# Fourth block of a retention-plus-MLP kernel: its chunks loaded in quarters, its first scores and k^T v' issued together

## The chip, the cores and the metric

One core of a Trainium2 chip. The metric is the device time of one execution in microseconds (us), the median of several runs. All time differences below are small beside the whole, so the profile is read in hundredths of a microsecond.

## The reference

Two stages in float32. The first is a recurrent retention over 768 tokens, for 4 batches and 8 heads of width 64; its output, 3072 tokens by 512, goes into an MLP with an ELU between its two layers.

```python
gamma = 1.0 - 2.0 ** (-5.0 - np.arange(H, dtype=np.float32))
for t in range(S):
    state = gamma[None, :, None, None] * state + np.einsum('bhd,bhe->bhde', k[:, :, t], v[:, :, t])
    y[:, :, t] = scale * np.einsum('bhd,bhde->bhe', q[:, :, t], state)
...
h = x @ w_in
g = np.where(h > 0.0, h, alpha * (np.exp(np.minimum(h, 0.0)) - 1.0))
return (g @ w_out).astype(np.float32)
```

## The kernel before

**Tiling.** The 3072 tokens are 24 chunks of 128 and six blocks of 512 (four chunks each, CPB = 4). The recurrence is computed in parallel form: per chunk, scores (q times k within 64 tokens, masked), states (sums of k^T v', where v' is v scaled by powers of gamma), and outputs. These matmuls use 64x64 tiles of the TensorE array; all MLP products use 128x128 tiles. The MLP's products are Strassen-like (seven products for eight), so each layer is a row of "products" that gather in PSUM banks named a, b and d, with sums by VectorE and copies by ScalarE between them.

**Order.** The order of every engine's instructions is the order of the program text (a manual schedule; no planner). Generators yield at certain points, and the loop around them puts side work into these points. The stage of the change is the second layer of the second block: `second_twice` (L954) runs seven outer products j in `ORDER2` (L804), each of seven inner products of 0.89 us. In its loop (L1802) every j from the second on gives three points, called "first", "middle" and "end" of a step; steps count from 1. From "first" to "middle" two products run, from "middle" to "end" one, from "end" to the next "first" four.

**Side work at these points.** The outputs of the third block's retention (`VISITS`, L1800), the loads of the fourth block's chunks (`LOADS`, L1801), and the fourth block's first pair of chunks: `scores(3, 0)` (L1818) at the end of step 4 and `states(3, 0)` (L1820) at the end of step 5. A run of 64x64 matmuls between 128x128 products is a visit. `scores` (L336) makes 64 profiled matmuls into two PSUM tiles, which VectorE masks into the chunk's k area; `states` (L385) makes 64 into two more and sums them (one copy by ScalarE, three additions by VectorE) in the chunk's area of plain k. All four PSUM tiles come from the pool of four, `ps_r` (L92).

**Chunks.** A chunk is a tile of 128 partitions x 2048 floats (1 MB): columns 0 to 1023 are q and k, turned; 1024 to 1535 are v; 1536 to 2047 are plain k. `load` (L114) takes one of four buffers (`ldpool`, L86) and issues the DMA on SP's queue (L125); `scale_v` (L299) scales v on GpSimd (POOL).

**Weights.** The weights of each inner product, 256 KB, come through a ring of 11 slots (L1776, L1777). When a product is issued, `done` (L857) frees its slot and `fetch` (L850) issues the next load, so a block is asked for about eleven products ahead. These loads, the chunk loads and the stores share SP's one queue, in program order. DMA completions are counted on eight semaphores in turn, and SP waits for the DMA issued eight before on the same one.

Of the kernel before, what the change touches and what calls it, by code (L numbers as in the profile page):

```python
# [28 lines left out]
def kernel(  # L29
# [47 lines left out]
    CPB = TB // C  # L77
# [34 lines left out]
    raw = {}  # L112

    def load(m, cuts=(0, 2048), behind=None):  # L114

        if m >= NCHUNK:
            return
        t = ldpool.tile([P, 2048], FP32, name="chunk", tag="chunk")
        raw[m] = (
            t[:, 0:1024].rearrange("p (a h c) -> p a h c", a=2, c=C),  # L120
            t[:, 1024:2048].rearrange("p (a h d) -> p a h d", a=2, d=D),
        )
        hold(t, behind)
        for lo, hi in itertools.pairwise(cuts):
            nc.sync.dma_start(t[:, lo:hi], qkv[m, :, lo:hi])  # L125

    def hold(t, other):

        if other is not None:
            nc.gpsimd.tensor_copy(t[0:1, 0:1], other[0:1, 0:1])  # L130
# [144 lines left out]
    powers_of(slice(0, 2 * C))  # L275

    load(0, (0, 1024, 1536))
    parts = load_piece_parts(2)
    next(parts)
    load(1, (0, 1536))  # L280
    next(parts, None)
    load_piece(staged[0][:, :, 0].bitcast(FP32))
    load(2, behind=raw[1][0][:, 0, 0])
    load(3, behind=staged[0][:, 512:, 0].bitcast(FP32))
    load_piece(staged[1][:, :, 0].bitcast(FP32))
# [13 lines left out]
    def scale_v(m, by_vector=False):  # L299
        if m >= NCHUNK:  # L300
            return
        i = chunks[m][1]
        v = raw[m][1][:, 0]
        eng = nc.vector if by_vector or m < 2 else nc.gpsimd
        eng.tensor_tensor(  # L305
            out=v, in0=v, in1=vf[:, i].unsqueeze(2).to_broadcast([C, H, D]), op=ALU.mult
        )
# [28 lines left out]
    def scores(tb, pp):  # L336

        sc = [ps_r.tile([P, 2, HP, D], FP32, name="sc", tag="r") for _ in range(2)]
        for x in range(2):
            score_products(sc, tb, pp, x)  # L340
        for a in range(2):
            nc.vector.tensor_tensor(
                out=raw[tb * CPB + 2 * pp + a][0][:, 1].rearrange("p h c -> p (h c)").rearrange("p (n t) -> p n t", t=D),
                in0=sc[a].rearrange("p x h t -> p (x h) t"),
                in1=cmask.unsqueeze(1).to_broadcast([P, 2 * HP, D]), op=ALU.mult,
            )
# [38 lines left out]
    def states(tb, pp):  # L385

        kvs = [ps_r.tile([P, 2, HP, D], FP32, name="kv", tag="r") for _ in range(2)]
        for x in range(2):
            state_products(kvs, tb, pp, x, range(2))
        for x in range(2):  # L390
            for sub in range(2):
                state_sum(kvs, tb, pp, x, sub)
# [284 lines left out]
    def send_small(count=None):  # L677
        for _ in range(min(count or len(to_send), len(to_send))):
            nc.sync.dma_start(*to_send.pop(0))
# [165 lines left out]
    def sent(j):  # L845
        send_small()
        blocked.discard((2, "t", j))
        fetch()
# [770 lines left out]
    def some(steps, count):  # L1619
        for _ in itertools.islice(steps, count):  # L1620
            pass
# [77 lines left out]
    def retention_step(tb, step):  # L1699
        if step == 0:  # L1700
            scores(tb, 0)
            scores(tb, 1)
        elif step == 1:
            states(tb, 0)
            states(tb, 1)
        else:
            outputs_step(tb, step - 2)
# [90 lines left out]
    flush()  # L1798
    retention_step(2, 2)
    step, VISITS = 0, {(1, "first"): 3, (1, "end"): 4}  # L1800
    LOADS = {(1, "first"): 0, (2, "end"): 1, (4, "end"): 2, (5, "end"): 3}  # L1801
    for s in sec:  # L1802
        if s == "first":
            step += 1
        at = (step, s if s in ("first", "middle") else "end")
        if s in ORDER2 and 1 <= step <= 4:
            some(smalls[1], 1 if step < 4 else 3)
        if step == 5:
            send_small(2)
        elif at == (6, "first"):  # L1810
            sent(1)
        if at in VISITS:
            retention_step(2, VISITS[at])
        if at in LOADS:
            load(3 * CPB + LOADS[at])
            scale_v(3 * CPB + LOADS[at])
        if at == (4, "end"):
            scores(3, 0)  # L1818
        elif at == (5, "end"):
            states(3, 0)  # L1820
        if s == ORDER2[-1]:
            break
# [8 lines left out]
    for nb in range(NB):  # L1831
# [40 lines left out]
        def bring(tb, n):  # L1872
            load(tb * CPB + n)
            scale_v(tb * CPB + n)
# [160 lines left out]
        step = 0  # L2035
# [3 lines left out]
        ]  # L2039
        LOADS = [(3, "middle"), (3, "end"), (4, "first"), (4, "middle")]  # L2040
        for s in sec:
# [5 lines left out]
            at = (step, s if s in ("first", "middle") else "end")  # L2047
            if more and at in VISITS:
                n = VISITS.index(at)
                retention_step(groups[n // 5], n % 5)  # L2050
            if more and at in LOADS:
                bring(groups[1], LOADS.index(at))
            if s == BIG2[-1]:
# [57 lines left out]
```

## Time and profile before

| what | value |
|---|---|
| median of 3 runs | 608.93 us (608.89 to 610.05) |
| the profiled execution | 609.02 us |
| its span | 607.2 us |
| TensorE busy | 600.0 us (99%) |
| VectorE / ScalarE / POOL busy | 507.7 / 261.5 / 97.4 us |
| DMA moved | 139.85 MB, 230 GB/s on average |
| HBM read / written | 105.12 / 33.82 MB |
| granted TensorE clock | 1.00 |

The span runs from the first to the last instruction; the profiled execution's time is 1.8 us longer. Times within the profile are counted from the span's start. PE is TensorE's matmul side, PEld its weight loads, DVE is VectorE, ACT ScalarE, SP the engine that issues all DMAs here. A line of the chain of waits reads: start in us, duration in us, engine, tile written, source line, number of instructions; "issue" in place of an engine is time in which the engine waited for nothing that the profile shows. A row for a stretch of time reads: from, to, length, then each engine's busy us and count, the granted clock, the share of time that the 16 DMA engines were busy, and GB/s. "DMA to landing" is the time from the issue of a DMA on SP to its completion. [...]

### The profile page before, as it was taken

The numbers are of one execution on the slowest core, as the hardware profiler recorded it, in microseconds if no ns is written. First come the engines' busy times: TensorE is split into PE (matmuls) and PEld (weight loads), VectorE is DVE, ScalarE is ACT, GpSimd is POOL, SyncE is SP. The second block draws the span as 40 slices with busy tenths as digits, with TensorE's granted clock in tenths as the row PEclk, the third lists the DMA queues.
The fourth block names the chain that finished last, engine by engine and source line by source line (L and its number), as shares of the span: only waits on it lengthen the run. The fifth ranks groups of instructions, "written<-read, shape, count | busy, mean of one in ns | idle before, by whom it ended". The sixth has DMA issues, their size and how long they took to land.

```text
span 607.2 us, 13751 instructions
## 1 busy us (share of the span) xinstructions
PE 600.0 (99%) x5510; PEld 492.7 (81%) x5510; DVE 507.7 (84%) x779; ACT 261.5 (43%) x448; POOL 97.4 (16%) x77
## 2 busy tenths in 40 slices
PE   8999999999999999999999999999999999999997
PEld 6865568888889999888766888888888866788886
DVE  5779889989899877989898787898658999779785
ACT  6898734205553112147589310100136679611110
POOL 1010000000230001000698000110000399000000
PEclk9999999999999999999999999999999999999999
DMA  8798579779968999599976545874564666556552
GB/s 316 277 400 298 173 225 266 234 239 272 345 223 268 298 374 314 185 308 279 358 252 208 128 134 156 270 274 119 187 171 155 168 222 194 158 153 189 151 154 114
DMA packets 85680, 139.85 MB, mean 230 GB/s; under 512 B 6896, under 2 KB 46576, under 8 KB 80880
## 3 DMA queue, kind: packets, MB, share of 16 engines
q1 hardware_dynamic: 85616, 138.96, 71.4%
q8 instruction: 44, 0.72, 0.5%
q14 instruction: 20, 0.16, 0.1%
HBM read 105.12 MB, written 33.82 MB: 229 GB/s over the span
## 4 chain that ended last, share of the span: by engine, by line
PE 98%; DMA 1%; DVE 0%; issue 0%
PE pa L1395 16%; PE pa L1286 9%; PE pd L1395 8%; PE pa L784 5%; PE pd L1286 5%; PE pa L978 4%; PE x L1349 4%; PE pb L1395 4%; PE pa L557 3%; PE x L647 3%; PE pb L1286 2%; PE pd L784 2%; PE pa L647 2%; PE pa L1336 2%; PE kv L371 2%; PE sc L331 2%
## 5 line engine op out<-in xcount | busy, mean ns | idle before, releaser
L1403 ACT COPY ms<-pa 128x256 f32<-128x256 f32 x41 | 15.2, 371 | 106.6 <-PE pa L1395 103.5
L1395 PE MATMUL pa<-gC,wq 128*128 128x256 f32 x240 | 56.8, 381 | 0.0
L1395 PEld LDWEIGHTS pa<-gC,wq 128*128 128x128 f32 x240 | 45.1, 190 | 7.3 <-issue 1.0
L305 POOL TENSOR_TENSOR chunk<-chunk,vf 128x512 f32<-128x512 f32 x15 | 18.9, 1270 | 154.4 <-DMA chunk<-in_qkv_dram 125.2
L1362 ACT ACTIVATE r<-r 128x512 f32<-128x512 f32 x64 | 40.4, 631 | 2.0
L1407 DVE TENSOR_TENSOR res<-pd,ms 128x256 f32<-128x256 f32 x26 | 11.0, 422 | 28.3 <-PE pd L1395 17.5
L1297 ACT COPY m<-pa 128x512 f32<-128x512 f32 x32 | 18.7, 584 | 34.8 <-PE pa L1286 31.6
L1395 PE MATMUL pd<-w_all,wq 128*128 128x256 f32 x120 | 28.3, 379 | 0.0
L1363 DVE SCALAR_TENSOR_TENSOR gC<-r,gC 128x512 f32<-128x512 f32 x24 | 27.9, 1169 | 0.0
L926 POOL TENSOR_TENSOR wp<-wp 128x512 fp32r<-128x512 f32 x6 | 8.8, 1468 | 117.1 <-DMA scratch_dram<-wi 102.7
L1395 PEld LDWEIGHTS pd<-w_all,wq 128*128 128x128 f32 x120 | 22.8, 190 | 3.1
L183 ACT ACTIVATE w_all<-wraw 128x1024 uint32<-128x1024 uint32 (+1 forms) x19 | 19.1, 1005 | 14.3 <-PE x L647 9.7
L1857 POOL TENSOR_TENSOR chunk<-chunk,w_all 128x512 f32<-128x512 f32 x4 | 5.1, 1284 | 124.7 <-ACT w_all L1297 124.7
L1377 DVE TENSOR_TENSOR gC<-w_all,gC 128x1024 f32<-128x1024 f32 x20 | 24.2, 1260 | 0.0
L1349 PE MATMUL x<-xl,wq 128*128 128x512 f32 x64 | 23.7, 457 | 0.0
L1395 PE MATMUL pa<-ts,wq 128*128 128x256 f32 x96 | 22.9, 381 | 0.0
L1395 PE MATMUL pa<-w_all,wq 128*128 128x256 f32 x96 | 22.9, 381 | 0.0
L185 ACT ACTIVATE w_all<-wraw 128x1024 fp8e4<-128x1024 f32 (+1 forms) x19 | 22.6, 1189 | 0.6
L1395 PE MATMUL pd<-ts,wq 128*128 128x256 f32 x96 | 22.7, 379 | 0.0
L557 PE MATMUL pa<-xb,w_all 128*128 128x512 f32 x48 | 21.5, 596 | 0.0
L1429 ACT COPY res<-pa 128x256 f32<-128x256 f32 x13 | 4.8, 372 | 38.1 <-PE pa L1395 38.1
L213 DVE CUSTOM_DVE_ANT_0 w_all<-wraw,w_all 128x2048 uint16<-128x2048 uint16 (+1 forms) x19 | 20.1, 1058 | 0.8
(369 smaller groups left out, 1599.3 us busy)
## 6 DMA issues: line engine op xcount, KB each, us to landing
wq<-scratch_dram SPq DMA_DIRECT2D x231, 256.0 KB, 3.4
chunk<-in_qkv_dram SPq DMA_DIRECT2D x22, 1024.0 KB, 7.5
wraw<-in_w_dram SPq DMA_DIRECT2D x15, 1024.0 KB, 5.7
scratch_dram<-wp SPq DMA_DIRECT2D x8, 512.0 KB, 3.8
out_dram<-res SPq DMA_DIRECT2D x7, 512.0 KB, 3.4
scratch_dram<-gT SPq DMA_DIRECT2D x12, 256.0 KB, 4.3
wq<-scratch_dram SPq DMA_DIRECT2D x24, 128.0 KB, 3.0
scratch_dram<-w_all SPq DMA_DIRECT2D x12, 256.0 KB, 3.0
```

Source lines behind the costliest of these rows:

```text
L185: nc.scalar.activation(top, hi.bitcast(FP32), AF.Copy, scale=2.0**-120, saturate=False)
L213: vec.tensor_tensor(out=flat, in0=c, in1=flat, op=ALU.add)
L557: nc.tensor.matmul(hp, lhsT=w[n][:, fi, j // 2, j % 2, :], rhs=xb[:, j, :], start=(j == 0), stop=(j == 3))
L647: nc.tensor.matmul(X[j][:, d, :], lhsT=w[j][:, d * P : d * P + P], rhs=x[j], start=(n == 0 and d == 0), stop=at_end, skip_group_check=True,)
L784: nc.tensor.matmul(ps[:, fi, :], lhsT=w[:, fi, j2, :], rhs=x[:, j2, :], start=(begin and fi == 0 and j2 == 0), stop=(j2 == 1), skip_group_ ...
L978: nc.tensor.matmul(ps, lhsT=w[:, f, :], rhs=ts[j][k][:, f, :], start=(begin and f == 0), stop=(f == 3), skip_group_check=True,)
L1286: nc.tensor.matmul(ps[:, f, :], lhsT=w[:, f, :], rhs=big_xs[j][k], start=(begin and f == 0), stop=True, skip_group_check=True,)
L1349: nc.tensor.matmul(joined(ps), lhsT=where[name][:, c : c + P].bitcast(F32R), rhs=x[:, k], start=(not third and c == 0), stop=(k == 1), ski ...
L1362: nc.scalar.activation(r, r, AF.Exp, scale=-1.0)
L1363: return lambda: nc.vector.scalar_tensor_tensor(g, r, -1.0, h, ALU.add, ALU.max)
L1377: nc.vector.tensor_tensor(out=quarter(to, r, t), in0=quarter(x, r, t), in1=quarter(y, r, t), op=op)
L1395: nc.tensor.matmul(ps, lhsT=w[:, f, :], rhs=ts[j][k][:, f // 2, f % 2, :], start=(begin and f == 0), stop=(f == 3), skip_group_check=True,)
```

## The change

The loads of the four chunks of the fourth block are cut into quarters of 512 columns, 256 KB each. They are issued one at a time, one at every point of steps 1 to 5 (two at the first), so that chunk 12 is issued over step 1, chunk 13 from the "first" of step 2 to that of step 3, chunk 14 up to the "middle" of step 4, chunk 15 from the end of step 4 to the end of step 5. The scaling of v is put behind the fourth quarter's issue. And `states(3, 0)` moves from the end of step 5 to the end of step 4, right behind `scores(3, 0)`, so that both are one visit of TensorE. On TensorE, VectorE, ScalarE and POOL the same instructions run as before; on SP there are twelve more DMA issues.

```diff
     def load(m, cuts=(0, 2048), behind=None):
+        for _ in load_parts(m, cuts, behind):
+            pass
+
+    def load_parts(m, cuts, behind=None):
 
         if m >= NCHUNK:
             return
...
         for lo, hi in itertools.pairwise(cuts):
             nc.sync.dma_start(t[:, lo:hi], qkv[m, :, lo:hi])
+            yield
...
-    LOADS = {(1, "first"): 0, (2, "end"): 1, (4, "end"): 2, (5, "end"): 3}
+
+    def quarter_loads():
+        for n in range(CPB):
+            for k, _ in enumerate(load_parts(3 * CPB + n, (0, 512, 1024, 1536, 2048))):
+                if k == 3:
+                    scale_v(3 * CPB + n)
+                yield
+
+    loads = quarter_loads()
...
-        if at in LOADS:
-            load(3 * CPB + LOADS[at])
-            scale_v(3 * CPB + LOADS[at])
+        if 1 <= step < 6:
+            some(loads, 2 if at == (1, "first") else 1)
         if at == (4, "end"):
             scores(3, 0)
-        elif at == (5, "end"):
             states(3, 0)
```

## The prediction

> **What bounds the kernel now.** Three views, from coarse to fine. The page first: TensorE is busy nearly everywhere, the chain that ended last is TensorE almost alone, and all matmul instructions reach it through one small DMA queue of 44 packets (q8; 44 blocks for some 11,250 matmul and weight-load records, so about 256 records in each).
>
> ```profile
> PE 600.0 (99%) x5510; PEld 492.7 (81%) x5510; DVE 507.7 (84%) x779; ACT 261.5 (43%) x448; POOL 97.4 (16%) x77
> DMA  8798579779968999599976545874564666556552
> q8 instruction: 44, 0.72, 0.5%
> PE 98%; DMA 1%; DVE 0%; issue 0%
> ```
>
> So time can only be won where TensorE stands still or pays for a change of tile shape. Second, the chain of waits in the stage of the change (215 to 232 us). It has three things to see: two gaps named "issue" (0.11 and 0.82 us), the two visits of 64x64 tiles (sc and kv, 1.09 us each), and the first product behind each visit at 1.09 us where the others take 0.89.
>
> ```profile
> 217.50 0.11 issue
> 217.61 1.13 PE pa L978 x8
> ...
> 219.63 0.89 PE pa L978 x8
> 220.52 1.09 PE sc L331 x64
> 221.62 1.09 PE pa L978 x8
> 222.70 0.89 PE pb L978 x8
> 223.60 0.56 PE pa L978 x5
> 224.16 0.82 issue
> 224.98 0.60 PE pa L978 x3
> ...
> 229.15 1.09 PE kv L371 x64
> 230.24 1.09 PE pa L978 x8
> ```
>
> After 26 us these two are the only gaps over 0.05 us on TensorE in the whole trace. Third, the DMA side of the same stage: the share of busy DMA engines by stretch of time, and issue to landing of the weight blocks that SP issued at 209 to 214 us.
>
> ```profile
> 197.00:212.00 15.00, 15.00 (x201) 14.74 (x194) 12.36 (x28) 2.12 (x8) 1.04 (x1) 1.00 0.91 297
> 212.00:228.00 16.00, 15.07 (x186) 14.53 (x185) 12.70 (x25) 2.39 (x9) 1.51 (x1) 1.00 1.00 372
> DMA to landing us min/median/max: 7.6/8.2/8.6
> ```
>
> The last two columns of the first two rows are DMA share and GB/s: the engines are full. Weight blocks issued at 209 us stand behind the 1 MB chunk that SP issued at 208.45 us. The single landings of the trace: chunk 13 lands at 216.14, the next weight block at 217.47, and then one block of 256 KB each 0.67 us (the queue is first in, first out). The product at 217.61 is the user of the block that landed at 217.47: the gap of 0.11 is data. The gap of 0.82 is not: it stops a product after 5 of its 8 matmuls, where no semaphore is waited for. Counted in TensorE's records it stands exactly at 19 x 256 + 193, and the next such point, 256 records on, is at 233.24 us, where the chain has 0.01 us of "issue". Between them lie fetches of 16 KB on q8: one ran from 222.54 to 223.49 and its first instruction started at 224.98 (1.49 behind the landing); the next ended at 231.90, used at 233.24 (1.34 behind). So TensorE ran out of instructions there, because the fetch stood behind the data queue: the block before it was entered about 214.3 us, 8 us before the fetch started.
>
> **The change, part by part.**
>
> *One visit instead of two.* Nothing is computed that was not before. A visit costs an entry and an exit. Elsewhere 128 such matmuls in one visit take 2.02 us (below), against 2 x 1.09 = 2.18: entry 0.16. The exit is the 1.09 of the next product against 0.89: 0.20. One visit less: -0.36 us. ACT's copy of a state (0.37 us; ACT is busy 2.39 of 16 us here) and VectorE's three sums (1.32 us) move forward with it.
>
> ```profile
> 172.66 2.02 PE sc L331 x128
> 174.68 1.92 PE pa L784 x8
> 176.60 1.73 PE pd L784 x8
> ```
>
> *Quarters instead of whole chunks.* Sixteen issues on SP in place of four: twelve more of 0.33 to 0.43 us, 4.6 us of SP spread over 33 us, in which SP mostly waits for freed slots. The bytes are the same. A queued 256 KB takes 0.67 us and a queued 1 MB about 2.50 (213.64 to 216.14), so a chunk costs 4 x 0.67 - 2.50 = 0.18 us more of DMA. [...]
>
> By SP's order the weight block that lands at 217.47 now has 7 quarters ahead of it instead of 8: 0.67 us earlier, gap gone: -0.11 (bounds -0.11 and, if the extra issues delay it, +0.3). Chunk 13 is complete one third of a step later than before in SP's order, at the latest about 220.5; its use by k^T v' in the merged visit is at 222.0. Its scaling on POOL (1.51 us) needs only the third quarter. Chunk 15, issued as a whole at 234.28 and landed at 242.10 for scores that start at 242.18, comes some 10 us earlier: no gap there before, no gain. All this hides under products of 0.89 us.
>
> *What the merged visit does to instruction fetch.* This decides. The block boundary does not move: the order of instructions up to the scores is unchanged. It falls 43 records into the k^T v' part, because that part now follows the scores at once. Scores start at 220.41 (without the 0.11), end at 221.5, and 43 of 128 records at 0.93 us per 128 are 0.31: TensorE needs the block at 221.8, not at 224.16. It had it at 224.98. If the fetch came as before, the gap would be 3.15 us. When will it come? From above: by SP's order the weight blocks issued around 214 to 216 us have one quarter more ahead of them than before (9 against 8), so the fetch behind them is 0.67 later: 225.65, gap 3.85. From below: SP runs at most eight transfers ahead (it waits for the landing of the one eight before, 14 such waits in this stage); eight quarter-sized ones are 5.3 us of queue, while before one of the eight was the big chunk. Then: entered 214.3 + 5.3 + 1.03 (the fetch began 1.03 behind the landing of the last block ahead of it, 221.51) + 0.95 + 1.45 = 223.05, gap 1.25. If the queue were short, gap 0. I take the middle of 223.05 and 225.65, 224.4, because both limits act on the same eight transfers: gap 2.6, against 0.82 before: +1.78. The next fetch is then needed about 10 us later (86 records of the visit, then 17 for each 0.89) and takes 8: no second gap.
>
> *VectorE.* Masks start at 224.07 (behind 3 us of other work) and the sums now follow them, 1.25 us ahead of the add that frees bank d, which in the trace ran at 226.51. With a gap of over half a us in the visit TensorE comes to that bank at 227.5 or later and the add is done by 227.0; without any gap it comes at 227.1: between 0 and +0.5, taken as 0.
>
> *Sum:* -0.36 - 0.11 + 1.78 = +1.31 us. The profiled execution took 609.02 (span 607.2 and 1.8 around it), 0.09 above the median of 608.93, so 610.3 by its own time and 610.2 by the median.
>
> **Rivals.** About 0.2% (1.2 us) is what a measurement of this kernel can tell from no change.
>
> 1. *Starved visit* (forecast): gap of 2.5 to 3.85 us, +1.2 to +2.6: 610.1 to 611.5. For it: the fetch of 222.54 was the latest of all 44 relative to its need, the next one was also just in time, and 256 records in 2.0 us leave no cover.
> 2. *The two halves cancel:* eight small transfers are a shorter queue, gap 1.25 (or up to 2.4): 1.25 - 0.82 - 0.11 - 0.36 = -0.04: 608.9, up to 610.1. For it: the 1 MB lump is what made 8.2 us of issue to landing; before it the same transfers took 4.0 to 5.9 us. Against: 12 more transfers in a full queue.
> 3. *No late fetch* (the other side): the fetch starts before 219.4 us and both gaps go: -0.36 - 0.11 - 0.82 = -1.29: 607.6; it turns faster below a gap of 0.1 us. For it: fetches in emptier stretches began 1 to 3 us after their block was entered. Against: the queue is full from 212 to 228 us. [...]
>
> **How the numbers follow.** Rival 1 has 0.48, rival 2 has 0.40 (nearly all within 0.2%), rival 3 has 0.12. The predicted time is that of rival 1 by the sum: 610.2, its own range 610.1 to 611.5. The range over all: from 607.6 (rival 3) to 611.6 (the upper bound of the gap with some tenths for the data wait). Faster 0.12, same 0.40, slower 0.48.
>
> **What would show it.** In the changed trace: sc and kv as one visit of 2.0 us of work around 220.4, with an "issue" gap inside it after about a third of kv; no gap at 217.5; the first product behind the visit at 1.09 and none at 229. The q8 fetch that begins near 222 must precede the end of the gap by 2.4 us. I am wrong if that fetch starts before 221.9 (rival 2) or before 219.4 (rival 3), or if the visit stops at its second half for chunk 13's last quarter, which would be a wait on data and not on instructions.

## The result, and the profile after

| | before | changed |
|---|---|---|
| median (22 executions each, one chip) | 609.19 us | 612.61 us |
| lowest and highest | 608.40 and 612.98 us | 609.06 and 616.83 us |
| the profiled execution | 609.02 us (span 607.2) | 612.23 us (span 610.5) |

The ratio is 1.0044, with a 95% interval of 1.0026 to 1.0061: slower by 1.6 to 3.7 us. (Ratios in this document leave out executions more than 1.5% above the fastest of the same kernel; of all runs below these are two of last_whole, 617.69 and 617.89 us.) The forecast was slower, 610.2 us (+1.3 on the 608.93 it knew), with a range of 607.6 to 611.6. The sign was right, the size (+3.4) was not.

The page of the profiled execution, in the lines that were shown of before:

```profile
PE 600.7 (98%) x5510; PEld 492.2 (81%) x5510; DVE 510.5 (84%) x779; ACT 262.1 (43%) x448; POOL 97.3 (16%) x77
DMA  8797678789977999599976445874555576546552
q8 instruction: 44, 0.72, 0.5%
PE 93%; DMA 4%; DVE 1%; issue 1%; ACT 0%; SPq 0%; DVEq 0%
```

TensorE's share of the chain fell from 98% to 93%, and DMA rose from 1% to 4%. The chain of waits in the stage of the change shows where:

```profile
217.38 0.89 PE pa L983 x8
218.27 0.97 PE pd L983 x8
219.25 0.89 PE pa L983 x8
220.14 1.09 PE sc L336 x64
221.23 0.93 PE kv L376 x64
222.16 1.09 PE pa L983 x8
...
225.04 0.84 PE pd L983 x8
225.88 5.73 DMA wq<-scratch_dram
231.61 0.02 issue
231.62 0.02 SPq L859
231.64 0.03 issue
231.67 5.67 DMA wq<-scratch_dram
237.34 0.14 issue
237.47 1.13 PE pa L983 x8
```

In this execution the one visit (sc and kv, 2.02 us) ran through: the gaps of 0.11 and 0.82 us are gone, and no fetch was late. The single packet of q8 that the forecast turned on began at 217.78 us, not at 222.54. In the last products before 235.90 us TensorE was 1.85 us ahead of before (the same matmuls compared). Then it stood still for 1.57 us, for the weight block of the stage's last product, and the products behind it were 0.04 us ahead. The chain says why the block was late: SP could issue it only at 231.67 us, 0.06 us after the landing of the transfer eight before it. The waits of TensorE from 200 to 340 us, by what ended them (total, times, longest):

```profile
PE pa L983 <- DMA wq<-scratch_dram: 1.6, 1, 1.6
PE x L1354 <- DVE x L923: 0.6, 2, 0.4
PE x L1354 <- DMA wq<-scratch_dram: 0.6, 1, 0.6
PE y L432 <- issue: 0.2, 1, 0.2
```

The second and third rows lie at 298 to 328 us, some 60 us behind the change. There this execution lost another 2.6 us against before, which no step of the forecast looked at. So the profile alone tells a story (a late last block, a loss in a later stage) that is not the forecast's. The next section shows that it is half of it.

### The profile page after: what moved, and what is told of

It reads as the page before. It is cut to its first block, busy times and chain, and to the rows that moved or that the text cites. A ratio compares the mean times of both kernels' runs of the same rounds, so it can differ in the third digit from the quotient of the medians.

```text
span 610.5 us, 13771 instructions
## 1 busy us (share of the span) xinstructions
PE 600.7 (98%) x5510; PEld 492.2 (81%) x5510; DVE 510.5 (84%) x779; ACT 262.1 (43%) x448; POOL 97.3 (16%) x77
## 4 chain that ended last, share of the span: by engine, by line
PE 93%; DMA 4%; DVE 1%; issue 1%; ACT 0%; SPq 0%; DVEq 0%
PE pa L1400 16%; PE pa L1291 9%; PE pd L1400 8%; PE pa L789 5%; PE pd L1291 4%; PE pb L1400 4%; PE x L1354 4%; PE pa L562 3%; PE pa L983 3%; DMA wq<-scratch_dram 3%; PE x L652 3%; PE pb L1291 2%; PE pd L789 2%; PE pa L652 2%; PE kv L376 2%; PE y L432 2%
## 5 line engine op out<-in xcount | busy, mean ns | idle before, releaser
L1368 DVE SCALAR_TENSOR_TENSOR gC<-r,gC 128x512 f32<-128x512 f32 x24 | 29.9, 1252 | 0.0
```

The source lines that it names most:

```text
L1368: return lambda: nc.vector.scalar_tensor_tensor(g, r, -1.0, h, ALU.add, ALU.max)
```

## The experiments

Times are of one set of executions each, beside executions of the kernel before on the same chip; the ratio is to those. "Clock" counts the executions whose mean granted clock was below 0.998 (about 3.4 us at half clock in one execution); for the kernel before it was 8 of 143. "Fetch" is the start of the q8 packet that was in dispute, "standstill" the longest of TensorE behind 200 us, both in the profiled execution.

| run | median us | ratio (95%) | clock | fetch us | standstill us |
|---|---|---|---|---|---|
| changed kernel | 612.61 | 1.0044 (1.0026 to 1.0061) | 10 of 22 | 217.78 | 1.57, block at 235.9 |
| merge_only | 613.13 | 1.0045 (1.0020 to 1.0071) | 7 of 12 | 222.16 | 2.67, in the visit |
| quarters_only | 610.75 | 1.0009 (0.9984 to 1.0033) | 2 of 12 | 222.59 | 0.48, at 332.2 |
| last_whole | 611.58 | 0.9999 (0.9970 to 1.0027) | 6 of 12 | 217.20 | 1.59, block at 296.8 |
| after_again | 612.33 | 1.0039 (1.0012 to 1.0066) | 8 of 12 | 221.01 | 2.02, in the visit |
| no_chunk13 | 610.05 | 1.0016 (0.9990 to 1.0042) | 3 of 12 | 218.91 | 0.44, at 241.7 |
| chunk13_early | 611.91 | 1.0035 (1.0010 to 1.0060) | 7 of 12 | 223.06 | 2.60, in the visit |
| before_later_chunk | 612.58 | 1.0038 (1.0016 to 1.0060) | 6 of 12 | 221.54 | 2.29, block at 302.6 |
| after_later_chunk | 612.64 | 1.0042 (1.0021 to 1.0064) | 4 of 12 | 217.77 | 1.89, block at 236.4 |
| before_early5 | 615.70 | 1.0077 (1.0052 to 1.0102) | 5 of 6 | 216.87 | 3.22, block at 281.3 |
| quarters12to14_early5 | 616.03 | 1.0101 (1.0057 to 1.0144) | 5 of 6 | 222.31 | 3.42, block at 281.0 |
| merged12to14_early5 | 615.07 | 1.0070 (1.0045 to 1.0096) | 8 of 10 | 218.23 | 3.28, block at 280.9 |
| after_early5 | 617.84 | 1.0109 (1.0079 to 1.0139) | 5 of 6 | 222.48 | 3.47, block at 285.2 |
| visit5_whole | 611.13 | 0.9989 (0.9964 to 1.0015) | 0 of 12 | 220.65 | 1.01, block at 297.1 |
| visit5_quarters12to14 | 611.10 | 1.0003 (0.9976 to 1.0030) | 4 of 12 | 218.79 | 2.01, chunk at 242.4 |
| before_spread5 | 610.34 | 0.9995 (0.9973 to 1.0016) | 3 of 12 | 222.06 | 0.14, at 242.2 |
| visit5_q_spread5 | 609.58 | 0.9976 (0.9956 to 0.9996) | 2 of 12 | 217.24 | 1.58, chunk at 241.0 |
| visit5_best | 607.73 | 0.9957 (0.9938 to 0.9977) | 0 of 12 | 217.17 | none |
| visit4_best | 609.35 | 0.9999 (0.9975 to 1.0023) | 5 of 12 | 216.81 | none |

The ratio is an estimate of its own and not the quotient of two medians: for visit5_whole it is 0.9989, where the medians (611.13, and 610.04 for before beside it) give 1.0018. Differences of a few tenths of a per cent between runs are read with that in mind.

### The two halves apart

**merge_only**

```diff
         if at == (4, "end"):
             scores(3, 0)
-        elif at == (5, "end"):
             states(3, 0)
```

> Chunk loads whole and where they were; only the fourth block's states move up behind its scores. Theory 1 (starved visit, the forecast): the fetch of instructions still starts near 222.5 us behind the whole chunk, the merged visit needs it at 221.9, so an issue gap of about 3.1 us stands inside the visit in place of 0.82 us: -0.36 + 2.3 = +1.9 us, 611.1 against 609.2. Theory 2 (late block: the quarters ahead of the stage's last weight block cost the time): no wait on a weight block near 237 us here, and no loss from it; if the fetch is not late either, -0.36 us, 608.8. Theory 3 (the loss is made at 297 to 330 us whatever the loads are): +1.5 to +2.6 us there too.

Measured: 613.13 us, ratio 1.0045. Theory 1's gap is what happened (2.67 us, expected near 3.1), but the time is 2 us above its 611.1. Chain of waits of merge_only around the visit:

```profile
220.58 1.09 PE sc L331 x64
221.67 0.34 PE kv L371 x21
222.01 2.67 issue
224.68 1.54 PE kv L371 x43
226.22 2.00 PE pa L978 x8
228.22 1.71 PE pb L978 x8
229.93 1.46 PE pa L978 x8
231.39 0.89 PE pd L978 x8
```

The visit stops after 21 of kv's 64 matmuls, which is 43 of its 128 records with the weight loads, and waits for no data ("issue"). But behind the gap stands something that nobody had forecast: 43 matmuls of kv take 1.54 us (0.93 x 43/64 = 0.62 is their share elsewhere), and three products take 2.00, 1.71 and 1.46 us in place of 1.09, 0.89 and 0.89. That is 0.92 + 0.91 + 0.82 + 0.57 = 3.2 us more. The rows by stretch of time name the cause in their granted clock (third figure from the right):

```profile
222.00:224.00 2.00, 0.01 (x1) 0.00 (x0) 2.00 (x4) 0.00 (x0) 0.00 (x0) 1.00 1.04 385
224.00:226.00 2.00, 1.32 (x43) 1.32 (x43) 1.41 (x3) 0.00 (x0) 0.00 (x0) 0.54 1.09 415
226.00:228.00 2.00, 2.00 (x14) 1.88 (x10) 1.27 (x3) 0.37 (x1) 0.00 (x0) 0.50 0.65 268
228.00:230.00 2.00, 2.00 (x12) 2.00 (x11) 0.00 (x0) 0.27 (x1) 0.65 (x1) 0.50 0.32 76
230.00:232.00 2.00, 2.00 (x15) 2.00 (x15) 0.29 (x1) 0.27 (x1) 0.39 (x1) 0.75 0.51 154
```

**quarters_only**

```diff
         if at == (4, "end"):
             scores(3, 0)
+        elif at == (5, "end"):
             states(3, 0)
```

(against the changed kernel)

> Sixteen quarters as in the changed kernel; the fourth block's states stay one step later. Theory 1 (starved visit): without the merged visit nothing is starved: gaps of 0.11 and 0.82 us gone, 608.3. Theory 2 (late block): both gaps gone up to 230 us, but the last weight block of the stage still lands near 237.3 us behind chunk 15's quarters, a wait of 1.1 to 1.6 us on it, so the early gain of 0.9 is lost again and more: 609.5 to 610.5, as far as the stage itself goes. Theory 3 (later stage): the same loss of 1.5 to 2.6 us at 297 to 330 us as in the changed kernel, 611 to 612.

Measured: 610.75 us, ratio 1.0009. No difference from before can be told, and the time lies between what theories 2 and 3 gave. In its profile the wait at 217.5 is gone and the fetch gap is 0.22 us. The last weight block landed at 236.85 and was used at 237.51: 0.66 us to spare in place of 2.91. So the quarters bring that block down to the edge, and it bites only a kernel that comes early. At 298 to 329 us this execution lost 3.3 us, as the first profile of the changed kernel lost 2.6.

**last_whole**

```diff
-        for n in range(CPB):
+        for n in range(CPB - 1):
...
+        if at == (5, "end"):
+            load(3 * CPB + 3)
+            scale_v(3 * CPB + 3)
```

(against the changed kernel)

> As the changed kernel (one visit, chunks 12 to 14 in quarters at the same points), but chunk 15 whole at the end of step 5, as before. Theory 1 (starved visit): no change to the changed kernel, 612.6. Theory 2 (late block): no quarter stands ahead of the last weight blocks; the wait of 1.57 us near 236 us goes, and the early gain of 1.3 us stays: 607.9 against 609.2. Theory 3 (later stage): the early gain stays, but 1.5 to 2.6 us are lost at 297 to 330 us: 609.4 to 610.5.

Measured: 611.58 us, ratio 0.9999. The median is 1.6 us above that of before beside it (609.96), so this ratio, which lacks the two longest executions, says less than it seems. The wait near 236 us is gone (1.33 us to spare), as theory 2 says; its 607.9 us did not come. In the profile TensorE was 1.39 us ahead of before at 230 us, and still 1.25 at 296 us. There it lost more than all of that: the waits of TensorE in last_whole from 176 to 340 us begin with

```profile
PE x L1354 <- DMA wq<-scratch_dram: 1.6, 1, 1.6
PE x L1354 <- DVE x L923: 1.4, 2, 1.1
```

Six of its twelve executions had the low clock, since it makes the same visit in the same place.

**after_again** is the changed kernel itself, once more.

> The changed kernel once more, for a second profile and more times. Theory 2 (late block): the wait on the last weight block near 236 us comes again, 1 to 2 us, and the gaps of 0.11 and 0.82 us are gone again. Theory 3: if the loss at 297 to 330 us (2.6 us in the first profile) is made by the change it comes again within 0.5 us; if it is variation between executions it differs by more than 1 us from the first profile, and the profile's own time with it.

Measured: 612.33 us, and a profile that is the opposite of the first one. Its chain of waits:

```profile
220.15 1.09 PE sc L336 x64
221.24 0.34 PE kv L376 x21
221.58 2.02 issue
223.60 0.91 PE kv L376 x43
224.51 1.59 PE pa L983 x8
226.10 1.71 PE pb L983 x8
227.81 1.21 PE pa L983 x8
```

Here the fetch began at 221.01, the visit starved for 2.02 us, and the clock fell behind it (0.62 over 224 to 228 us). There was no wait for the last weight block, because TensorE came to it 2.0 us later than before, and no loss at 297 to 330 us. So the same program has executions of two kinds. Over both sets the changed kernel ran 34 times: 18 with the low clock, median 613.4 us, and 16 without, median 610.5. Of these 16, nine lie at 609.1 to 610.6 and seven at 612.2 to 614.5, the latter where the first profile lies. That both halves of the loss, the starved visit and the later stage, come in only some executions is why no single profile showed it whole. The low clock is a sign of the starved visit, not a count of it: quarters_only, without the merged visit, has it in 2 of 12 executions.

### What the fetch waits for, and what the later stage waits for

**no_chunk13** (merge_only, with zeros written by GpSimd in place of chunk 13's load)

```diff
-            load(3 * CPB + LOADS[at])
+            load(3 * CPB + LOADS[at], (0,) if LOADS[at] == 1 else (0, 2048))
+            if LOADS[at] == 1:
+                a_, b_ = raw[3 * CPB + 1]
+                nc.gpsimd.memset(a_, 0.0)
+                nc.gpsimd.memset(b_, 0.0)
```

> The merged visit with whole loads, but chunk 13 is not loaded: GpSimd writes zeros in its place (so the fourth block is computed from zeros there). This takes 1 MB out of the DMA queue ahead of the late fetch and leaves TensorE's instructions as in merge_only. Theory S (the visit is starved because the fetch stands behind the full data queue, and a standstill of 2 us or more is followed by about 3.5 to 7 us of clock at 0.5): the fetch that started at 222.16 us in merge_only starts before 219.5 us, no gap over 0.5 us in the visit, clock 1.00 in most executions, and the median falls by 2 to 4 us from 613.1 to 609 to 611 (the rest being the loss at 297 to 330 us, which this kernel does not touch). Rival (the fetch is late by itself or the visit is slow by its shape): gap of 2 to 2.7 us again and 613.

Measured: 610.05 us, ratio 1.0016, against merge_only's 613.13 and 1.0045. The fetch began at 218.91 and the visit ran through. The row for 218 to 224 us of merge_only:

```profile
218.00:224.00 6.00, 4.01 (x109) 3.75 (x107) 4.39 (x8) 0.53 (x2) 0.06 (x1) 1.00 1.04 379
```

and of no_chunk13:

```profile
218.00:224.00 6.00, 6.00 (x165) 5.81 (x164) 4.45 (x9) 0.96 (x4) 0.00 (x0) 1.00 0.85 245
```

With the DMA engines at 0.85 in place of 1.04, TensorE is busy 6.00 of 6 us in place of 4.01, in the profiled executions. Three of twelve executions had the low clock in place of seven of twelve. The intervals of the two ratios overlap (up to 1.0042 here, from 1.0020 there). And an early fetch is no proof of an emptier queue: in visit4_best, described below, the fetch began earlier still, at 216.81 us, with the DMA engines as full as in merge_only:

```profile
218.00:224.00 6.00, 6.00 (x163) 5.81 (x163) 4.85 (x9) 1.17 (x4) 0.00 (x0) 1.00 1.04 376
```

So that the full data queue delays the fetch, as the forecast and theory S had it, is not shown.

**chunk13_early** (merge_only, chunk 13 at another point)

```diff
-    LOADS = {(1, "first"): 0, (2, "end"): 1, (4, "end"): 2, (5, "end"): 3}
+    LOADS = {(1, "first"): 0, (2, "first"): 1, (4, "end"): 2, (5, "end"): 3}
```

> As merge_only, but chunk 13 is loaded at the first point of step 2, three weight blocks earlier in SP's order. Theory S: the queue is empty of the 1 MB load some 2.7 us earlier, so the fetch starts near 219.5 us in place of 222.16; needed at 221.9 and usable 2.4 us behind its start, so a gap of 0 to 0.6 us, too short for the clock to fall: median 609 to 611. Rival (the fetch waits for its own reasons, not for the chunk): gap of 2 to 2.7 us and clock at 0.5 again, median 613.

Measured: 611.91 us; 2.60 us in the visit, fetch at 223.06. The expectation of theory S fell: with the load moved by three blocks the fetch was no earlier, and the DMA share over 218 to 224 us was 1.04, as in merge_only. TensorE now waited for weight blocks at 214.7, 216.0 and 218.3 us (0.17 to 0.23 us each), which stand behind the chunk.

**before_later_chunk** and **after_later_chunk** (before and changed kernel, the fifth block's second chunk three weight blocks later in SP's order)

```diff
-            if more and at in (5, 6):
-                load(groups[0] * CPB + at - 5)
+            if more and at in ((5, 7) if nb == 0 else (5, 6)):
+                load(groups[0] * CPB + (at > 5))
```

> The kernel before, with one edit far behind the change: the second chunk of the fifth block is loaded one turn (three weight blocks) later, so that the blocks used near 298 us stand ahead of it. Theory L (some executions lose 2 to 3 us at 297 to 330 us because that weight block is late and VectorE's sums then fall together with POOL's): the executions of before between 610 and 613 us become rare, median 608.4 to 608.9 against 609.2 to 610. Rival (the loss there is something else): the spread of 608 to 613 stays and the median within 0.3 us.

> The changed kernel with the same edit. Theory L: of its executions, those with clock 1.00 at 612 to 614.5 us go to 608 to 610; those with a starved visit (clock 0.997 or lower) stay at 611.5 to 613. Median between 609.5 and 612. If S is the whole cost and L none: median 612.4 as before this edit. If L is the whole cost: 608.5 to 609.5 with no execution over 611.

Measured: 612.58 and 612.64 us. Both failed to gain: the wait did not go, it moved to the block that now stands behind the chunk. The waits of TensorE in before_later_chunk begin with

```profile
PE pa L1349 <- DMA wq<-scratch_dram: 2.3, 1, 2.3
```

and the row behind that wait shows a clock of 0.50 again, with nothing of the change in this kernel:

```profile
306.00:308.00 2.00, 2.00 (x6) 1.54 (x5) 0.09 (x1) 1.83 (x4) 2.00 (x2) 0.50 0.85 288
```

This separates the slow clock from the visit: a standstill of 2.29 us on data was followed by it too. after_later_chunk had the early fetch, and with it the late last block once more, 1.89 us at 236.4.

### A failed cure

Four kernels load the fifth block's first two chunks near 260 us in place of 281 and 289: the kernel before (before_early5), the kernel with chunks 12 to 14 in quarters and two visits (quarters12to14_early5), the same with one visit (merged12to14_early5), and the changed kernel (after_early5).

```diff
-            if at == 2:
+            if at == 2 and nb:
...
-            if more and at in (5, 6):
-                load(groups[0] * CPB + at - 5)
+            if nb == 0 and at == 1:
+                held_x = [ldpool.tile([P, 2048], FP32, name="chunk", tag="chunk") for _ in range(2)]
...
+                load(groups[0] * CPB)
+                load(groups[0] * CPB + 1)
+            if more and nb and at in (5, 6):
+                load(groups[0] * CPB + at - 5)
```

> The kernel before, with the fifth block's first two chunks loaded near 259 us, where the DMA queue is half empty, in place of 281 and 289 us. In the stage of the change nothing differs. Theory L (some executions lose 2 to 3 us at 297 to 330 us, since the weight blocks used there land behind these two chunks with 0 to 1.2 us to spare): the wait near 298 us goes, the spare time of that block rises from 1.2 to over 3 us, executions of 610 to 613 us become rare, median 608.3 to 608.9. Rival (that loss comes from VectorE and POOL alone): spread and median as before, 609.2 to 610.

> The same edit with chunks 12 to 14 in quarters as in the changed kernel, chunk 15 whole where it was, and the fourth block's states one step later as before: two visits. Theory S: two visits leave the fetch time enough, so its gap stays under 0.9 us and the clock at 1.00; with L's wait gone too, the 0.1 to 0.9 us that the quarters win is kept: 607.7 to 608.6, below before. Rival (the quarters cost DMA time whatever is done): 609 to 611.

> The same with one visit (scores and states together at the end of step 4). It differs from the run beside it by the merge alone. Theory S: where the fetch is early (before 219 us) 607.4 to 608.0, where it is late (after 220.9 us) a gap of 2 to 2.7 us and clock at 0.5 behind it, 611 to 613; both kinds in one set of executions, median 1.5 to 4 us above the two-visit kernel. Rival (the merge costs nothing and the quarters are the cost): within 0.5 us of the two-visit kernel.

> The changed kernel with the fifth block's first two chunks early. Theory S plus L plus the late last block: executions with an early fetch pay the wait of 1.6 to 1.9 us on the last weight block of the stage and nothing at 297 us: 608.5 to 609.5; those with a late fetch 611.5 to 612.7; none of the clock-1.00 executions above 610.5. If L plays no part in the changed kernel's 612.6, the clock-1.00 executions stay at 612 to 613.

Measured: 615 to 618 us, all four worse. The waits near 298 us did go in all four profiles, but 22 stores and two weight blocks stand between the two loads and the weight block needed near 280 us in SP's order: that block was issued at 282.18 us in place of 276.53, and its spare time had been 0.85 us. The waits of TensorE in before_early5 begin with

```profile
PE pa L1286 <- DMA wq<-scratch_dram: 3.2, 1, 3.2
```

The pair that was to give the cost of the merge (615.07 with one visit, 616.03 with two) says nothing, since the wait at 281 us can absorb what came before it.

### The visit moved, and the waits taken away one by one

**visit5_whole** (merge_only) and **visit5_quarters12to14** (last_whole) have the one visit four products later:

```diff
-        if at == (4, "end"):
+        if at == (5, "first"):
             scores(3, 0)
             states(3, 0)
```

> Whole loads; scores and states of the fourth block in one visit, but at the first point of step 5, four products later than in merge_only. The block boundary then falls 107 records into the visit's 256, and TensorE needs the fetched block near 224.8 us in place of 221.9. Theory S (place against fetch): even a fetch that starts at 222.5 is usable at 224.98, so a gap of 0 to 0.3 us there, up to 1.2 us at the next boundary near 232 us, no slow clock: 608.5 to 610, 3 to 4 us under merge_only's 613.1. Rival (a merged visit costs 2 to 4 us wherever it stands): 612 to 613.

> The same place of the one visit, chunks 12 to 14 in quarters as in the changed kernel, chunk 15 whole where it was before. Theory S: no gap over 1.2 us near 224 and 232 us, clock 1.00, the two early gaps of before gone: up to 1.3 us ahead at 240 us. What is left of it at the end depends on the loss at 297 us (theory L, which this kernel doesn't touch): 608 to 611. Rival (quarters or merge cost the time wherever they stand): 612 and more.

Measured: 611.13 and 611.10 us, 1.1 us above before beside them (610.04), with both ratios about 1. The median of visit5_whole missed theory S's 608.5 to 610, but its ratio is 0.9989 against merge_only's 1.0045, with intervals that do not overlap. It differs from merge_only by the place of the visit alone: none of its twelve executions had the low clock, against seven of twelve. At 230 us TensorE was 1.46 us ahead of before. Then it lost 0.53 us waiting for chunk 15 at 241 and 1.01 us at 297, with 0.8 us of waits for VectorE behind that. In visit5_quarters12to14's profile the wait for chunk 15 was 2.01 us and was followed by a clock of 0.63 and 0.74: a wait on data, with the same slow clock behind it.

**before_spread5** (before) and **visit5_q_spread5** (visit5_quarters12to14) load the fifth block's second and third chunks near 304 and 313 us:

```diff
-            if more and at in (5, 6):
+            if more and at in ((5,) if nb == 0 else (5, 6)):
                 load(groups[0] * CPB + at - 5)
...
-            if more and n in (2, 5):
-                load(groups[0] * CPB + 2 + n // 5)
+            if more and n in ((1, 3, 5) if nb == 0 else (2, 5)):
+                load(groups[0] * CPB + (n // 2 + 1 if nb == 0 else 2 + n // 5))
```

> The kernel before, with the fifth block's second and third chunks loaded later (16 and 6 weight blocks later), near 304 and 313 us, where the blocks have 4 to 8 us to spare. Theory L: the block used near 298 us has over 3 us to spare in place of 1.2 and the wait there goes in all executions: 608.3 to 608.9, executions over 610 rare. Rival (VectorE and POOL lose the time whenever the blocks come): spread of 608 to 613 and median of 609 to 610.5 stay.

> visit5_quarters12to14 and before_spread5 in one. If S and L are both right this keeps the early gain of about 1 us to the end: 607.5 to 608.5, under the kernel before. If only S is right: as visit5_quarters12to14. If neither: 611 to 613.

Measured: 610.34 and 609.58 us. In the profiles the block of 298 us has 2.07 and 3.04 us to spare in place of 1.21, and nothing waits there. But the median of before_spread5 is no better than before's (ratio 0.9995, 0.9973 to 1.0016): the expectation of 608.3 to 608.9 fell, and what scatters the kernel before between 608 and 613 us is not settled by it. visit5_q_spread5 is faster than before by its ratio, 0.9976, but by no more than 0.5 us in the medians, and it missed its 607.5 to 608.5. Its one wait left was for chunk 15, 1.58 us.

**visit5_best** takes that away (chunk 15 one point earlier, behind the stage's last weight blocks and ahead of two small stores); **visit4_best** is visit5_best with the visit where the changed kernel has it.

```diff
+        if at == (5, "middle"):
+            load(3 * CPB + 3)
+            scale_v(3 * CPB + 3)
         if step == 5:
             send_small(2)
...
-        if at == (5, "end"):
-            load(3 * CPB + 3)
-            scale_v(3 * CPB + 3)
```

> visit5_q_spread5 with chunk 15 issued one point earlier, ahead of two small stores and behind the stage's last weight blocks. Theory: the wait of 1.58 us for chunk 15 near 241 us falls to under 0.3 us, no other new wait, so the 1.56 us by which TensorE is ahead at 230 us stays: 607.4 to 608.3, under the kernel before by 0.2 to 0.4%. Rival (something later takes it, as three times so far): 609 to 610 as visit5_q_spread5.

> visit5_best with the one visit at the end of step 4, where the changed kernel has it. Theory S (place against fetch): executions of two kinds, with an early fetch as visit5_best, 607.5 to 608.5 at clock 1.00, and with a late one a gap of 2.0 to 2.7 us after 43 matmul-and-load records of k^T v' and clock 0.997 or lower, 610.5 to 613; about half of each, so a median 1 to 4 us above visit5_best. Rival (the place is nothing): within 0.5 us of visit5_best, hardly any execution at clock 0.997 or lower.

Measured: 607.73 us for visit5_best, ratio 0.9957 (0.9938 to 0.9977), as expected, under the kernel before and under the changed kernel; its twelve executions lie between 607.05 and 609.57 us, all at full clock. Its chain has the one visit, no gap, and no product over 1.09 us:

```profile
222.84 0.97 PE pd L983 x8
223.81 1.09 PE sc L336 x64
224.90 0.93 PE kv L376 x64
225.84 1.09 PE pa L983 x8
226.92 0.89 PE pd L983 x8
```

visit4_best has a median of 609.35 us. Its twelve executions are of two kinds, as expected, though not quite at the expected times: seven without the low clock, 607.3 to 610.1 us, and five with it, 609.2 to 613.4. Its profiled execution (607.31 us) is of the first kind. Between the two stands only the place of the visit: 1.6 us of median, and five executions in place of none with the low clock.

## Why the prediction was right or wrong

**The starved visit: right in what stops TensorE, and in about half of the executions.** The place was exact (43 records into k^T v', in four profiles of kernels with the visit there), the length was 2.02 to 2.67 us against 2.6 forecast. In each of the four, kv went on 1.46 to 1.63 us after the packet had landed, much as in before (1.49 and 1.34). So TensorE stood still for lack of instructions; why the packet came late is not shown. In the changed kernel itself the packet began at 217.78 and 221.01 us, both before the 221.9 that the forecast named as its sign of being wrong, and the one gap, 2.02 us, is rival 2's (1.25 to 2.4) by length. Gaps of 2.5 us and more were seen in after_early5, merge_only and chunk13_early.

**"Gap 2.6, against 0.82 before: +1.78": the step that failed, a term of the sum that was mis-sized.** It counted the standstill and nothing behind it. A standstill of that length was not paid once. Behind it the granted clock was 0.50 for 3.4 us (after_again) or 6.8 (merge_only), as worked out below. In after_again that is 0.29 us on kv (0.91 against 0.62) and 0.50 + 0.82 + 0.32 on three products, 1.9 us in all, and 3.2 us in merge_only. With it the term is +3.1 (2.02 - 0.82 + 1.9) to +5.1 us (2.67 - 0.82 + 3.2). The page of before had a clock of 1.00 throughout and, behind 26 us, no gap over 0.82 us, so that trace could not price this; the sum took the clock of 1.00 for given without saying so. Here a standstill of 2.01 us (visit5_quarters12to14) was enough for a clock of 0.50 behind it, and one of 1.89 us (after_later_chunk) was not.

**The fetch's time, "I take the middle of 223.05 and 225.65": wrong as a single number.** It is one of two. In the 20 profiles of this case the packet began ten times at 216.8 to 218.9 us and ten times at 220.6 to 223.1, and the changed kernel itself had one of each. So a starved visit and no late fetch (rival 3) were no alternatives: both happen in one program. Rival 3, given a chance of 0.12, describes up to 235 us the kind of execution that half of the profiles caught. The lower bound also starts from a block "entered about 214.3"; by the same count of records (which includes semaphore instructions) the first record of that block ran at 215.4 us, which would put this bound at 224.2, and kv in after_again went on at 223.60.

**"All this hides under products of 0.89 us": wrong for the last weight block of the stage.** The forecast followed chunk 13 and 15 to their users, and not the weight blocks that the extra issues push back. Before, eight transfers ahead of the last block stood chunk 14, which had landed at 228.90 us; with a quarter of chunk 15 more in the row it is a weight block that lands at 231.61, itself 2.0 us later than before. The last block is issued at 231.67 in place of 229.76. Before, it lay there 2.91 us ahead of its use; now it lands at 237.34, 1.44 us after TensorE was ready for it. The wait takes 1.8 us from an execution that had won 1.85. This is the limit of eight transfers that the forecast used for the fetch and forgot here. (All 431 transfers in the profile of before landed in the order of their issue.) last_whole shows it: with chunk 15 behind that block the wait is gone.

**The sum stopped at 242 us.** What is won there meets, at 297 us, a weight block that had 1.21 us to spare in the profile of before. In the profiles of last_whole and visit5_whole TensorE was still 1.25 and 0.91 us ahead of before at 296 us, and behind the wait for that block (1.59 and 1.01 us) it was 0.60 and 0.36 us late. The sums of VectorE behind it then fall beside POOL's: the rows of VectorE's operation with two SBUF inputs, from 296 to 330 us, in before,

```profile
L1363 DVE SCALAR_TENSOR_TENSOR gC<-r,gC 128x512 f32<-128x512 f32 x9 | 11.9, 1332 | 0.0
```

and in the first profile of the changed kernel,

```profile
L1368 DVE SCALAR_TENSOR_TENSOR gC<-r,gC 128x512 f32<-128x512 f32 x9 | 14.0, 1559 | 0.0
```

are 2.1 us apart over nine instructions; single ones take 0.68 to 2.4 us, all of them beside operations of POOL. In the whole profile of before the six of these operations that no operation of POOL overlaps took 680 to 683 ns, and the 18 that one overlaps 684 to 2249, 1331 on average; in that of the changed kernel they took 679 to 685 ns, and 683 to 2365, 1442 on average. So beside POOL they took about twice as long on average; no run here changed POOL's work to show it by itself.

**Merge of two visits, "-0.36": right.** Where the fetch is early, the visit is one piece of 2.02 us, with one product of 1.09 behind it and none at 229 us. **The gap at 217.50, "-0.11": right that it goes, too small.** The product behind it took 1.13 us in before and 0.89 now, so this wait had cost 0.35 us. The gap of 0.82 likewise cost 1.09, since its product took 0.56 and 0.60 us around it in place of 0.89. With the 0.36 of the merge that is 1.80 us, near the 1.85 by which TensorE was ahead before the last block, where rival 3 gave 1.29. **VectorE taken as 0: right** in this stage; no wait on it appears there. **"No second gap" behind the visit: right** as far as 240 us.

What stays open: why the fetch begins in two groups of times, whether the data queue delays it, and what scatters the kernel before between 608 and 613 us, since before_spread5 took away the one wait that the profiles offered for it. How the 612.6 us divides between the starved visit and the later stage is known only by the count of executions above.

## What to carry to other kernels

A gap is not worth its length alone: ask whether it is long enough for TensorE's clock to fall (here 2.01 us was, and 1.89 was not), and count the slow microseconds behind it (here 3.4 or 6.8 at a clock of 0.50). Before instructions are packed more densely, find where their blocks end and how long each fetch then has; the same visit four products later was not interrupted in any of its four profiles. And where all transfers share one queue with a fixed number under way (eight here), an edit's gain is worth only the smallest spare time of a weight block behind it (0.85 us near 280 us and 1.21 near 297 us here), so list that spare time through the later stages, not just for the buffers that the edit touches.

## What was not expected of the hardware

- **The clock fell behind standstills of 2.01 us and more.** Over all profiles of this case, behind 200 us: eight standstills of 1.0 to 1.9 us were followed by a clock of 1.00; of ten from 2.01 to 3.5 us nine were followed by a clock of 0.50, at a price of 1.9 us (after_again) and 3.2 us (merge_only) where it was counted. Among the nine are waits for instructions, for weight blocks and for a chunk. The one without it lasted 3.42 us (quarters12to14_early5); its page has no row for the clock, but 20 matmuls ran in the 4.00 us behind it (284.38 to 288.38 us), where it was 12 to 14 in the other three early5 kernels. The length of the slow stretch can be worked out from the rows: in merge_only 0.54 over 2 us is 1.84 us at half clock, then 4 us at 0.50, then 0.75 over 2 us is 1 us, together 6.8; in after_again 0.62 over 4 us is 3.0 us and 0.91 over 2 us 0.4, together 3.4. One length is twice the other.
- **The slow stretch lasts 3.4 us or twice that, and does not begin where the standstill ends.** By the rows with finer bounds the clock was 0.50 from 224.96 to 228.36 us in after_again and from 224.16 to 231.00 in merge_only, and 1.00 on either side. Worked out so from the rows, seven of the nine slow stretches lasted 3.40 to 3.44 us and two 6.84 and 6.85 (merge_only, merged12to14_early5). They began between 1.25 us before the end of the standstill (merged12to14_early5) and 1.40 us behind it (before_early5). What sets their start, and why the standstill of 3.42 us had none behind it, is not shown.
- **The start of one fetch comes in two groups** 1.7 to 6.3 us apart over the 20 profiles; the changed kernel alone had one of each (217.78 and 221.01 us). In 18 of 20 profiles the early group goes with a fetch before it that began after 206.0 us, the late group with one before that. Why was not tried.
- **A 256 KB load takes a place in the row of eight like a 1 MB load.** Four quarters moved the same bytes, but the weight block behind them had to wait for a later landing: the stage's last block was issued 0.06 us behind the landing of the transfer eight before it at 231.61 us, where before that transfer was the 1 MB chunk 14, landed at 228.90, and the block was issued at 229.76.
